# Turning every normed row tile of the later quarters by DMA from two queues, with three more weight units held in SBUF, in a recurrent-memory attention plus MLP kernel

## The chip, the core and the metric

One core of a Trainium2 chip. The metric is the device time of one execution in microseconds (us). Engines are named as in the profile: PE (TensorE; PEld is its weight loads), DVE (VectorE), ACT (ScalarE), POOL (GpSimd) and SP (SyncE, which here only issues DMAs). ACTq, SPq and POOLq are the rows of the DMA issues and waits of these engines' instruction streams.

## The reference, cut to what matters

```python
xn = layernorm(x)                                    # x: 2048 x 1024, bf16
mem = mem0                                           # 8 x 1024
for s in range(64):                                  # 64 segments of 32 rows
    h = concat(mem, xn[32*s : 32*s+32])              # 40 rows
    q, k, v = h @ Wq, h @ Wk, h @ Wv                 # 32 heads of 128
    p = softmax(mask(q @ k.T / sqrt(128)))
    o = (p @ v) @ Wo                                 # 40 x 1024
    mem, out[32*s : 32*s+32] = o[:8], o[8:]
out = x + out + gelu(xn @ w1 + b1) @ w2 + b2         # hidden size 3584
```

## The kernel before

**Two parts.** First comes the MLP for all rows, then the 64 segments, which depend on each other through `mem`. The attention weights are cut into 64 units of 512 KB. 47 of them are resident in SBUF, the other 17 of each segment come again every segment (`start_stream`): 15 through DMAs from copies in DRAM (`Wc_...`) into a ring of six SBUF places, two from PSUM banks. A stream slot is filled again as soon as PE is done with it (`unit_done`).

**The MLP goes in four quarters of 512 rows** (`tg` 0 to 3; four row tiles of 128 rows each). A quarter has 28 groups of the first product (`first_product`, L523, eight matmuls each), each followed by the gelu on ACT and DVE (L594, L598 to L602, and `gelu_tail` L582, L583), and then the second product (L643, or L674 in the last quarter): per row tile `t` two groups of 28 matmuls, and after each two additions on DVE (L650, L651). The finished row tile goes to DRAM (`keep_R`, L473).

**The next quarter's input is made beside the second product.** Its four row tiles are normed (`ln_stats`, `ln_sqrt`, `ln_rstd`, `ln_apply`: L401 to L420) and turned, so that the model dimension lies on the partitions; the turned tile pair is `xnT`. The first product of the next quarter reads all four turned tiles at once. In the kernel before, row tiles 1, 2 and 3 are turned by DMA (`send_x`, L448: eight `dma_start_transpose` of 32 x 512 per row tile, all issued by ACT), and row tile 0 by PE (`turn_x`: eight transposes L429, then copies L434 on DVE and ACT), placed on PE between `t` 2 and `t` 3. `ln_xn` has two buffers, so the third tile's `ln_apply` waits until the first tile's DMAs have read it.

**Order.** Every engine's order is the order written in the program (a manual schedule); the layer below only puts in semaphore waits, by the regions of SBUF and DRAM that instructions read and write. On SP stand, at the end of a quarter: the four `keep_R`, the loads of x for the quarter after next, in quarter 0 the copies of the streamed units to DRAM and the first five resident units (`EARLY`), then `keep_xT` (L456, L466; the latter wait for POOL's copies L461), then `turn_R` (L510: 52 or 56 small DMAs from DRAM to DRAM that bring the quarter's rows into the segments' layout). `turn_R` is issued by SP in quarters 0 and 1 and by POOL in quarter 2; the last quarter's rows go in pieces during segments 1 to 4.

**Weights during the last quarter.** As `w1`, `w2` and gelu places fall free, units are fetched into them (`fetch_resident`), in the order of `RES_PLACES`. Units that find no place are in `LATE`: five of them (tiles `W_O_...`), fetched in segment 0 one at a time, each behind a streamed unit, as are `xt2` and `xt3`.

**Segment 0** (`first`) has `sums(0)` (the row sums of the softmax) behind unit 7 of the second Q half pass; the others have it behind unit 4.

Of the kernel before, what the change touches and what calls it, by code (L numbers as in the profile page):

```python
# [10 lines left out]
BF16 = mybir.dt.bfloat16  # L11
# [6 lines left out]
P = 128  # L18
S = 2048
DM = 1024  # L20
# [38 lines left out]
SUMS_0 = (4, 4, 4, 4)  # L59
# [59 lines left out]
def kernel(  # L119
# [16 lines left out]
    nc = tc.nc  # L136
# [48 lines left out]
    def slab(place):  # L185
        if place in low:
            return low[place]
        return slabs.tile([P, 2048], BF16, name="u", tag=place)
# [39 lines left out]
    NP1 = FC // 2  # L228
    RING = ["xn0", "xn1", "w1_0", "w1_1", "xn2", "xn3"]
    assert len(RING) == STREAM_BUFS  # L230
    EARLY = list(low) + ["spare0", "spare1"]
    RES_PLACES = EARLY + ["xt0", "xt1"] + [f"w1_{k}" for k in range(2, NP1)]
    for k in range(7):
        RES_PLACES += [f"w2_{2 * k}", f"w2_{2 * k + 1}", f"gT{k}"]
    UNIT_AT = dict(zip(RES_PLACES, RESIDENT))
# [18 lines left out]
    def fetch_resident(*places):  # L254
        for place in places:
            unit = UNIT_AT[place]
            res_tiles[unit] = slab(place)[:, :]
            fetch(res_tiles[unit], unit)
# [88 lines left out]
    with tc.tile_pool(name="ma", bufs=2) as ma:  # L347
# [39 lines left out]
        for i in range(14):  # L387
            t = slab(f"w2_{i}")[:, :].rearrange("p (c d) -> p c d", d=DM)
# [5 lines left out]
        rstd = ma.tile([P, NT], F32, name="ln_rstd", bufs=1)  # L394

        half_stats = {}

        def ln_half(tt, c):
            if c == 0:
# [5 lines left out]
        def ln_stats(tt):  # L405
            ln_half(tt, 0)
            ln_half(tt, 1)

        def ln_sqrt(t0, t1):
            nc.scalar.activation(  # L410
                out=rstd[:, t0:t1], in_=mv[:, t0:t1, 1:2].rearrange("p t o -> p (t o)"), func=ACT.Sqrt,
                bias=eps_t[:, :], scale=1.0,
            )

        def ln_rstd(t0, t1):
            nc.vector.reciprocal(out=rstd[:, t0:t1], in_=rstd[:, t0:t1])

        def ln_apply(tt):
            xn = ma.tile([P, DM], BF16, name="ln_xn")
            nc.vector.tensor_scalar(  # L420
                out=xn[:, :], in0=xtoks[tt], scalar1=mv[:, tt, 0:1], scalar2=rstd[:, tt:tt + 1],
                op0=ALU.subtract, op1=ALU.mult,
            )
            return xn

        def turned(xn):
            pT = new_ps("pT")
            for kt in range(KT):
                nc.tensor.transpose(pT[:, kt, :], xn[:, kt * P:(kt + 1) * P], ident)  # L429
            return pT  # L430

        def turned_out(tt, pT, half, xnT, cp):
            t = tt % 4
            cp(  # L434
                out=xnT[half][:, 4 * t:4 * t + 4, :, :].rearrange("p s k t -> p k s t"),
                in_=pT[:, 4 * half:4 * half + 4, :].rearrange("p k (s t) -> p k s t", t=SEG),
            )

        def turn_x(tt, xn, xnT):
            pT = turned(xn)  # L440
            for half in range(2):
                turned_out(tt, pT, half, xnT, nc.scalar.copy if (tt + half) % 2 else nc.vector.tensor_copy)

        def send_x(t, xn, xnT):

            for i in range(4):
                for half in range(2):
                    nc.scalar.dma_start_transpose(  # L448
                        out=xnT[half][:, 4 * t + i, :, :],
                        in_=xn[SEG * i:SEG * i + SEG, 512 * half:512 * half + 512],  # L450
                    )
# [67 lines left out]
        xnT = new_xnT(0)  # L519
# [47 lines left out]
        for tg in range(4):  # L567
            last = tg == 3
            if last:

                load_x_rows(0)
                load_left_rows(0)
                h = 4 * IN_BANKS[1] + 2 * IN_BANKS[2]
                nc.sync.dma_start(out=kq[:, 0:DM], in_=Wo_v[:, h, :])
                start_stream("xn0")
                start_stream("xn1")
                fetch_resident("xt0", "xt1")
            gts = [slab(f"gT{i}")[:, :].rearrange("p (c t) -> p c t", c=4) for i in range(7)]

            def gelu_tail(fb, u, xb):  # L580
                sg = ma.tile([P, 512], BF16, name="g_sg")
                nc.scalar.activation(out=sg[:, :], in_=u[:, :], func=ACT.Sigmoid, scale=GELU_C)  # L582
                nc.vector.tensor_tensor(out=gts[fb // 4][:, fb % 4, :], in0=sg[:, :], in1=xb[:, :], op=ALU.mult)  # L583

            pend = None
            for fb in range(FC):
                if tg == 0 and fb < len(begun):
                    ps = begun[fb]
                    first_product(ps, fb, xnT, 8, 16)
                else:  # L590
                    ps = new_ps()
                    first_product(ps, fb, xnT, 0, 16)
                xb = ma.tile([P, 512], BF16, name="g_xb", bufs=3)
                nc.scalar.activation(  # L594
                    out=xb[:, :], in_=ps[:, :], func=ACT.Identity, bias=b1col[:, fb:fb + 1], scale=1.0
                )
                u = ma.tile([P, 512], BF16, name="g_u")
                nc.vector.tensor_tensor(out=u[:, :], in0=xb[:, :], in1=xb[:, :], op=ALU.mult)  # L598
                nc.vector.tensor_scalar(
                    out=u[:, :], in0=u[:, :], scalar1=0.044715, scalar2=1.0, op0=ALU.mult, op1=ALU.add  # L600
                )
                nc.vector.tensor_tensor(out=u[:, :], in0=u[:, :], in1=xb[:, :], op=ALU.mult)  # L602
                if pend is not None:
                    gelu_tail(*pend)
                pend = (fb, u, xb)
                if last and fb == MEM_AT:
                    put_mem(o_sb, nxt["hT"], new_ps(), wide=False)
                    nc.sync.dma_start(out=d_oL[:, 0:DM], in_=Wo_v[:, h + 1, :])
                if last and fb % 2:
                    place = f"w1_{fb // 2}"  # L610
                    if place in RING:
                        start_stream(place)
                    else:
                        fetch_resident(place)
            gelu_tail(*pend)

            if tg == 0:
                for nb in range(2):
# [4 lines left out]

            if not last:
                xnT = new_xnT(tg + 1)
                for t in range(4):
                    ln_stats(4 * tg + 4 + t)
                ln_sqrt(4 * tg + 4, 4 * tg + 8)
                ln_rstd(4 * tg + 4, 4 * tg + 8)
                for t in (1, 2):  # L630
                    send_x(t, ln_apply(4 * tg + t + 4), xnT)
                for t in range(4):
                    ttg = 4 * tg + t
                    if t == 1:
                        send_x(3, ln_apply(4 * tg + 7), xnT)
                    if t == 2:
                        xn = ln_apply(4 * tg + 4)
                    rsb = xtoks[ttg]
                    for nb in range(2):
                        cs = slice(nb * 512, (nb + 1) * 512)  # L640
                        ps = new_ps()
                        for fc in range(FC):
                            nc.tensor.matmul(  # L643
                                ps[:, :],
                                lhsT=gts[fc // 4][:, fc % 4, t * P:(t + 1) * P],
                                rhs=w2_sb[fc // 2][:, fc % 2, cs],
                                start=(fc == 0),
                                stop=(fc == FC - 1),
                            )
                        nc.vector.tensor_tensor(out=ps[:, :], in0=ps[:, :], in1=b2bc[:, cs], op=ALU.add)  # L650
                        nc.vector.tensor_tensor(out=rsb[:, cs], in0=ps[:, :], in1=rsb[:, cs], op=ALU.add)  # L651
                        if nb == 1 and t == 2:
                            turn_x(4 * tg + 4, xn, xnT)
                    keep_R(ttg, rsb)
                xtoks.update({tt: load_x(tt) for tt in range(4 * tg + 8, min(4 * tg + 12, NT))})
                if tg == 0:
# [2 lines left out]
                    fetch_resident(*EARLY)  # L659
                keep_xT(tg + 1, xnT)  # L660
                for t in range(4):
                    turn_R(4 * tg + t, nc.gpsimd if tg == 2 else nc.sync)
            else:


# [51 lines left out]
    with tc.tile_pool(name="late", bufs=1) as late:  # L717
# [66 lines left out]
        for s in range(NSEG):  # L784
            g, i4 = divmod(s, GRP)
            first, final = s == 0, s + 1 == NSEG
# [113 lines left out]
            def q_left(u):  # L900

                if i4 >= 2 + u and more:
                    q = qS[:, i4 - 2 - u, :, :]
                else:
                    q = qL[u][:, :, NL * i4:NL * i4 + NL]
                nc.vector.tensor_copy(out=q_home[:, :, 0:NL], in_=q)
# [197 lines left out]
            at = {} if first else {1: [lambda: q_left(0)]}  # L1104
# [7 lines left out]
            if left_q[0] and not first:  # L1112
# [5 lines left out]
            at = {  # L1118
                0: [lambda: nc.vector.transpose(out=nat_home, in_=nat_home)],
            }  # L1120
            at[7 if first else SUMS_0[i4]] = [lambda: sums(0)] + ([] if first else [lambda: q_left(1)])
            if left_q[1] and not first:
                at[0].insert(0, lambda: keep_q(1))
            if left_k[1]:
# [56 lines left out]
            for n, unit in enumerate(O_UNITS):  # L1181
                t = unit_tile(unit)
# [115 lines left out]
```

## Time and profile before

| | |
|---|---|
| Median of 3 runs | 1794.47 us (1789.17 to 1797.13) |
| The profiled execution | 1797.63 us, of which the span of its trace is 1795.9 us |
| MLP | 0 to about 404 us of the span; quarters' first products from about 12, 111.86, 210.05 and 307.19 us |
| Segments | from about 404 us to the end |
| PE busy | 1701.3 us (95%) |
| DVE, ACT, POOL busy | 984.2, 683.8, 300.4 us |
| DMA | 594.43 MB, mean 331 GB/s |

Rows of the trace give start and length in us of an instruction or of a run of equal ones; a number in brackets is the idle time before it, with what ended it. `x24` means 24 instructions. In a table of windows each engine's busy time in the stretch is followed by its count; then come the granted PE clock (1.00 is full speed), the mean busy share of the 16 DMA engines and their GB/s.

### The profile page before, as it was taken

The page shows a single profiled execution, that of the slowest core. Times are in us where ns is not written, and L with a number is a line of the kernel's source. Part 1 is how long each engine was busy: PE and PEld are TensorE (multiplying, and loading weights), DVE is VectorE, ACT ScalarE, POOL GpSimd, SP SyncE. Part 2 cuts the span into 40 slices and gives each one's busy share as a digit, 9 for nine tenths or more (in the row PEclk, how much of TensorE's full clock was granted, in tenths as well). Part 3 has the DMA queues.
Part 4 walks back from the last instruction along what each step waited for, and adds up shares of the span by engine and source line. Part 5 has one row for each costly group of instructions (what it writes and reads, how often), then busy time and mean ns, then how long its engine had stood idle before and what let it go on. Part 6 is the DMA issues. An engine that isn't in the chain of part 4 may idle for free.

```text
span 1795.9 us, 71439 instructions
## 1 busy us (share of the span) xinstructions
PE 1701.3 (95%) x31065; PEld 892.2 (50%) x31085; DVE 984.2 (55%) x2514; ACT 683.8 (38%) x1692; POOL 300.4 (17%) x586
## 2 busy tenths in 40 slices
PE   8999999998998999999999999999999999999998
PEld 4444444444455554555555555454555454555554
DVE  7657483825554555555555555555555555555554
ACT  6334261603333333333333434333334343434333
POOL 0000002401231111111121212111112111111211
PEclk9999999999999999999999999999999999999999
DMA  9455222779999999999999999999999999999998
GB/s 284 137 149 185 73 62 64 258 246 380 377 389 367 368 380 375 387 389 376 387 389 374 386 375 396 378 382 379 385 380 385 380 374 384 394 371 393 390 393 321
DMA packets 232830, 594.43 MB, mean 331 GB/s; under 512 B 57715, under 2 KB 88035, under 8 KB 232516
## 3 DMA queue, kind: packets, MB, share of 16 engines
q1 hardware_dynamic: 197584, 567.08, 84.3%
q0 software_dynamic: 16896, 16.85, 2.9%
q10 hardware_dynamic: 18036, 5.94, 1.3%
q8 instruction: 243, 3.98, 0.9%
q14 instruction: 71, 0.58, 0.1%
HBM read 573.43 MB, written 28.90 MB: 335 GB/s over the span
## 4 chain that ended last, share of the span: by engine, by line
PE 76%; DMA 12%; DVE 4%; ACT 4%; issue 3%; ACTq 1%; POOL 0%; DVEq 0%; POOLq 0%; SPq 0%
PE acc L811 38%; PE acc L1069 13%; PE ps L523 11%; DMA u<-Wc_O 7%; PE ps L643 7%; DMA u<-Wc_V 4%; PE ps L674 3%; ACT mixed L980 1%; PE acc L1020 1%; PE mixed L928 1%; DVE kq L895 1%; ACTq L448 1%; DVE pd_main L993 1%; DMA u<-Wc_K 1%; ACT kq L890 1%
## 5 line engine op out<-in xcount | busy, mean ns | idle before, releaser
L811 PE MATMUL acc<-u,hr_home 128*32 128x512 bf16 x11520 | 761.1, 380 | 18.9 <-issue 10.8
L811 PEld LDWEIGHTS <-hr_home 128*32 128x32 bf16 x12288 | 348.6, 96 | 287.9 <-issue 39.4
L811 PE MATMUL acc<-u,hrL 128*32 128x512 bf16 x2880 | 255.6, 380 | 4.1 <-DVE qL L863 2.0
L523 PE MATMUL ps<-u 128*128 128x512 bf16 (+1 forms) x920 | 196.2, 376 | 0.0
L271 DVE TENSOR_SCALAR u<-kept 128x512 uint32<-128x512 uint32 x254 | 163.2, 685 | 55.5 <-PE acc L811 40.7
L863 ACT CAST d_oL<-acc 128x512 bf16<-128x512 f32 x143 | 82.0, 584 | 264.2 <-PE acc L811 252.1
L1069 PEld LDWEIGHTS <-kq 128*32 128x32 bf16 x3908 | 106.2, 99 | 80.6 <-issue 23.9
L643 PE MATMUL ps<-u 128*128 128x512 bf16 x657 | 145.2, 379 | 0.8
L523 PEld LDWEIGHTS <-u 128*128 128x128 bf16 x920 | 90.5, 99 | 103.6
L1069 PE MATMUL acc<-u,d_oL 128*32 128x512 bf16 x1944 | 133.3, 381 | 7.5 <-DMA u<-Wc_O 4.5
L1069 PE MATMUL acc<-u,kq 128*32 128x256 bf16 (+1 forms) x2372 | 119.9, 319 | 14.4 <-DMA u<-Wc_O 12.2
L993 DVE TENSOR_TENSOR pd_main<-kq,mixed 128x320 bf16<-128x320 bf16 x128 | 62.5, 488 | 128.9 <-ACT mixed L980 127.9
L895 DVE STREAM_TRANSPOSE kq<-kq 128x512 bf16<-128x512 bf16 x128 | 91.0, 711 | 72.5 <-ACT kq L890 70.5
L890 ACT CAST kq<-acc 128x512 bf16<-128x512 f32 (+2 forms) x192 | 85.4, 445 | 111.0 <-PE acc L811 81.4
L1260 POOL DMA_DIRECT2D out_dram<-hr_home x168 | 85.4, 516 | 221.6 <-DVE hr_home L1227 221.4
L867 ACT CAST kq<-acc 128x512 bf16<-128x512 f32 x128 | 75.2, 588 | 111.7 <-PE mixed L934 109.9
L811 PEld LDWEIGHTS <-hrL 128*32 128x32 bf16 x3072 | 88.4, 96 | 58.2 <-issue 5.0
L958 DVE TENSOR_TENSOR kq<-kq,mixed 128x96 bf16<-128x96 bf16 (+1 forms) x256 | 38.1, 190 | 121.6 <-ACT kq L948 67.8
L643 PEld LDWEIGHTS <-u 128*128 128x128 bf16 x672 | 65.5, 98 | 78.8 <-DVE g_u L602 0.4
L594 ACT ACTIVATE g_xb<-ps,b1col 128x512 bf16<-128x512 f32 x112 | 76.8, 686 | 71.0 <-PE ps L523 70.4
L980 ACT ACTIVATE mixed<-mixed,small_consts 128x160 f32<-128x160 f32 x256 | 94.2, 368 | 8.4
L1069 PEld LDWEIGHTS <-d_oL 128*32 128x32 bf16 x2592 | 66.5, 96 | 62.2 <-issue 16.8
(127 smaller groups left out, 1987.6 us busy)
## 6 DMA issues: line engine op xcount, KB each, us to landing
u<-Wc_K SPq DMA_DIRECT2D x256, 512.0 KB
u<-Wc_V SPq DMA_DIRECT2D x256, 512.0 KB
u<-Wc_O SPq DMA_DIRECT2D x256, 512.0 KB
u<-Wc_Q SPq DMA_DIRECT2D x192, 512.0 KB
u<-in_B_w_dram SPq DMA_DIRECT2D x28, 512.0 KB
u<-in_A_Wq_dram SPq DMA_DIRECT2D x13, 512.0 KB
u<-in_A_Wv_dram SPq DMA_DIRECT2D x12, 512.0 KB
u<-in_A_Wk_dram SPq DMA_DIRECT2D x9, 512.0 KB
```

Source lines behind the costliest of these rows:

```text
L271: nc.vector.tensor_single_scalar(out=out, in_=in_, scalar=0, op=ALU.bitwise_or)
L523: nc.tensor.matmul(ps[:, SEG * s0:SEG * s1].rearrange("p (s t) -> p s t", t=SEG), lhsT=w1_sb[fb // 2][:, kt, (fb % 2) * P:(fb % 2 + 1) * P ...
L594: nc.scalar.activation(out=xb[:, :], in_=ps[:, :], func=ACT.Identity, bias=b1col[:, fb:fb + 1], scale=1.0)
L643: nc.tensor.matmul(ps[:, :], lhsT=gts[fc // 4][:, fc % 4, t * P:(t + 1) * P], rhs=w2_sb[fc // 2][:, fc % 2, cs], start=(fc == 0), stop=(fc ...
L811: nc.tensor.matmul(o, lhsT=lhs[:, i, :], rhs=m, start=(i == seq[0]), stop=(i == seq[-1]), tile_position=(0, 32 * j),)
L863: cp(out=out, in_=ps.rearrange("p (h e) -> p h e", e=32))
L890: nc.scalar.copy(out=q_home[:, h0:h1, NL:40], in_=ps[:, 32 * h0:32 * h1].rearrange("p (h e) -> p h e", e=32))
L895: nc.vector.transpose(out=home, in_=home)
L980: nc.scalar.activation(out=mixed[:, 160 * b:160 * b + 160], in_=mixed[:, 0:160], func=ACT.Exp, scale=-1.0, bias=off[:, b:b + 1],)
L993: nc.vector.tensor_tensor(out=pdA.rearrange("p c b q -> p b c q"), in0=prA[:, None, :, :].to_broadcast([P, 2, 4, 40]), in1=dd, op=ALU.mult,)
L1069: nc.tensor.matmul(acc[r0:r0 + rows, 0:256 * len(blocks)], lhsT=lhsT, skip_group_check=True, rhs=o_columns(t, k, blocks), start=start, sto ...
L1260: loads.dma_start(out=out_flat[rows, 256 * j:256 * j + 256], in_=res[32 * j:32 * j + NX, :])
```

## The change

- All four row tiles of quarters 1 to 3 are turned by DMA. `send_x` takes the engine that issues: tiles 0 and 2 from SP, tiles 1 and 3 from ACT. `turn_x`, with its PE transposes and its copies, is gone (the first quarter keeps its own turning by PE).
- Statistics, square root and reciprocal go by pairs of row tiles. Tile 0 is sent behind the first square root, tile 1 behind both; tiles 2 and 3 are normed and sent in front of `t` 1 and `t` 2 of the second product.
- The normed tiles and the gelu's small tiles lie in three 4 KB slabs (`late2`, `late0`, `late1`) that later hold weight units. So 43 instead of 40 units have a place of `RES_PLACES`, and `LATE` has two units instead of five. `late2` is fetched early in the last quarter, `late0` and `late1` behind its last gelu. `g_xb` has four buffers instead of three.
- `turn_R` is issued by POOL in quarters 0 and 1 too.
- `sums(0)` of segment 0 stands behind unit 4 instead of 7.

```diff
-    RES_PLACES = EARLY + ["xt0", "xt1"] + [f"w1_{k}" for k in range(2, NP1)]
+    RES_PLACES = EARLY + ["late2", "xt0", "xt1"] + [f"w1_{k}" for k in range(2, NP1)] + ["late0", "late1"]
...
+        xn_place = slab("late2")
+        xns = deque(xn_place[:, DM * k:DM * k + DM] for k in range(2))
+        small_places = [slab("late0"), slab("late1")]
+        parts = [small_places[k // 4][:, 512 * (k % 4):512 * (k % 4) + 512] for k in range(8)]
+        xbs, us, sgs = deque(parts[0:4]), deque(parts[4:6]), deque(parts[6:8])
...
-            xn = ma.tile([P, DM], BF16, name="ln_xn")
+            xn = next_of(xns)
...
-        def turn_x(tt, xn, xnT):
-            pT = turned(xn)
-            for half in range(2):
-                turned_out(tt, pT, half, xnT, nc.scalar.copy if (tt + half) % 2 else nc.vector.tensor_copy)
-
-        def send_x(t, xn, xnT):
+        def send_x(t, xn, xnT, eng):
             for i in range(4):
                 for half in range(2):
-                    nc.scalar.dma_start_transpose(
+                    eng.dma_start_transpose(
                         out=xnT[half][:, 4 * t + i, :, :],
                         in_=xn[SEG * i:SEG * i + SEG, 512 * half:512 * half + 512],
                     )
...
-                fetch_resident("xt0", "xt1")
+                fetch_resident("late2", "xt0", "xt1")
...
             gelu_tail(*pend)
+            if last:
+                fetch_resident("late0", "late1")
...
-                for t in range(4):
-                    ln_stats(4 * tg + 4 + t)
-                ln_sqrt(4 * tg + 4, 4 * tg + 8)
-                ln_rstd(4 * tg + 4, 4 * tg + 8)
-                for t in (1, 2):
-                    send_x(t, ln_apply(4 * tg + t + 4), xnT)
+                t0 = 4 * tg + 4
+
+                def norms(a):
+                    for tt in range(t0 + a, t0 + a + 2):
+                        ln_stats(tt)
+                    ln_sqrt(t0 + a, t0 + a + 2)
+                    ln_rstd(t0 + a, t0 + a + 2)
+
+                norms(0)
+                send_x(0, ln_apply(t0), xnT, nc.sync)
+                xn = ln_apply(t0 + 1)
+                norms(2)
+                send_x(1, xn, xnT, nc.scalar)
                 for t in range(4):
                     ttg = 4 * tg + t
-                    if t == 1:
-                        send_x(3, ln_apply(4 * tg + 7), xnT)
-                    if t == 2:
-                        xn = ln_apply(4 * tg + 4)
+                    if t in (1, 2):
+                        send_x(t + 1, ln_apply(t0 + t + 1), xnT, (nc.sync, nc.scalar)[t - 1])
...
-                        if nb == 1 and t == 2:
-                            turn_x(4 * tg + 4, xn, xnT)
...
-                    turn_R(4 * tg + t, nc.gpsimd if tg == 2 else nc.sync)
+                    turn_R(4 * tg + t, nc.gpsimd)
...
-            at[7 if first else SUMS_0[i4]] = [lambda: sums(0)] + ([] if first else [lambda: q_left(1)])
+            at[4 if first else SUMS_0[i4]] = [lambda: sums(0)] + ([] if first else [lambda: q_left(1)])
```

More of the change, by code (lines that the diff above doesn't have):

```diff
@@ L396, with next_of @@
         half_stats = {}
+        xn_place = slab("late2")
[3 more added lines that the diff above has]
+        xbs, us, sgs = deque(parts[0:4]), deque(parts[4:6]), deque(parts[6:8])
+        def next_of(ring):
+            ring.rotate(-1)
+            return ring[-1]
         def ln_half(tt, c):
@@ L576 @@
                 start_stream("xn1")
-                fetch_resident("xt0", "xt1")
+                fetch_resident("late2", "xt0", "xt1")
             gts = [slab(f"gT{i}")[:, :].rearrange("p (c t) -> p c t", c=4) for i in range(7)]
             def gelu_tail(fb, u, xb):
-                sg = ma.tile([P, 512], BF16, name="g_sg")
+                sg = next_of(sgs)
                 nc.scalar.activation(out=sg[:, :], in_=u[:, :], func=ACT.Sigmoid, scale=GELU_C)
@@ L592 @@
                     first_product(ps, fb, xnT, 0, 16)
-                xb = ma.tile([P, 512], BF16, name="g_xb", bufs=3)
+                xb = next_of(xbs)
                 nc.scalar.activation(
@@ L596 @@
                 )
-                u = ma.tile([P, 512], BF16, name="g_u")
+                u = next_of(us)
                 nc.vector.tensor_tensor(out=u[:, :], in0=xb[:, :], in1=xb[:, :], op=ALU.mult)
```

## The prediction

> **What bounds the kernel now.** I read the page's slices first, then windows around the end of the MLP, then the timeline at each quarter's end. Every chance below is against 0.5%, about 9 us, which is what a measurement of this kernel can tell from no change.
>
> ```profile
> PE   8999999998998999999999999999999999999998
> ...
> DMA  9455222779999999999999999999999999999998
> ```
> ```profile
> 345.00:360.00 15.00, 14.95 (x70) 6.84 (x70) 12.68 (x35) 9.07 (x15) 8.39 (x16) 1.00 0.66 197
> 360.00:404.00 44.00, 43.79 (x202) 19.86 (x203) 11.46 (x17) 1.17 (x2) 1.67 (x3) 1.00 0.72 244
> ...
> 412.00:440.00 28.00, 23.59 (x482) 12.46 (x478) 13.71 (x33) 6.69 (x20) 5.12 (x10) 0.94 1.04 401
> ```
> The columns behind the stretch are PE, PEld, DVE, ACT and POOL busy, clock, DMA share, GB/s. In the MLP (first nine slices) PE alone is full: 14.95 of 15 and 43.79 of 44 us, with a third of the DMA time free. From 412 us on it is the other way: DMA share 1.04 at 401 GB/s, PE 4.4 us idle of 28; later windows show a share of 0.99 to 1.01 up to 1700 us. So an MLP delay moves the end one for one, and bytes taken out of the segments shorten them. Now the first quarter's end, in order of time:
>
> ```profile
> 63.05 36.43 PE L643 MATMUL ps<-u 128*128 128x512 bf16 x164
> ...
> 68.36 0.21 DVE L403 BATCH_NORM_AGGREGATE ln_mv<-ln_stats 128x2 f32<-128x12 f32 x1
> ...
> 72.52 32.10 ACTq L448 DMA_TRANSPOSE u<-ln_xn  x24
> ...
> 84.05 0.55 DVE L420 TENSOR_SCALAR ln_xn<-u,ln_mv,ln_rstd 128x1024 bf16<-128x1024 bf16 x1 [7.27 <-DMA u<-ln_xn]
> ...
> 94.41 0.55 DVE L420 TENSOR_SCALAR ln_xn<-u,ln_mv,ln_rstd 128x1024 bf16<-128x1024 bf16 x1 [5.55 <-DMA u<-ln_xn]
> ...
> 99.77 12.25 PE L643 MATMUL ps<-u 128*128 128x512 bf16 x55
> ...
> 111.86 2.32 PE L523 MATMUL ps<-u 128*128 128x512 bf16 x10
> ```
> Three tiles' 24 DMA turns take 32.1 us of ACT's queue and end at 104.6 us, 7 us before PE wants them. The third and fourth L420 waited for a buffer, so 84.05 and 94.41 are when the first and the second tile had been read and landed.
>
> **Part 1: four turns in a row instead of three in a stream.** One turn:
>
> ```profile
> L448 ACTq DMA_TRANSPOSE u<-ln_xn x1: 1257/1257/1257, 81.6 to 81.6; - x1
> ```
> This is the eighth issue, from the trace in a window of 0.5 us: it ends at 82.9, 10.3 us behind the first, and its landing is seen at 84.05. So a tile takes 11.5 us from first issue to landing (third quarter: 268.53 to 279.96, 11.4). In one queue the next tile doesn't wait for that landing: 94.41 less 84.05 is 10.4.
>
> In the changed kernel's built order the first transpose of each later tile waits for all eight DMA semaphores, that is for the landing of the tile before it, because it is issued from the other queue. The four turns then stand one behind another: 4 x 11.5, and three hand-overs through eight semaphore waits of 17 ns, 0.15 each: 46.5 us. The trace of before has one stream only and can't show two. The Trainium skill, page "DMA: Bandwidth & Descriptors", section "Silent corruption: two transposing streams in flight at once", speaks against this change: the later stream's first transpose must wait for the earlier stream's full completion count. By that rule the wait can't be removed and the sum is the one made here; if the two queues ran side by side, as no run here shows, all tiles would be there some 23 us earlier and this part would cost nothing.
>
> The chain starts earlier than before, as only two tiles are normed first. From the end of the last aggregate to ACT's first issue were 1.16 us (71.36 to 72.52); the second aggregate ends at 68.57, so SP starts at 69.7 and the last tile has landed at 116.2. The first product began at 111.86: 4.3 us later. Second quarter: aggregate end 166.35, start 167.5, landed 214.0 against 210.05: 4.0. Third: 264.55, 265.7, 312.2 against 307.19: 5.0. Sum **13.3 us**. The second product itself would end at 111.6, 208.8 and 307.0, so PE idles 4.6 to 5.2 us each time. Between ends: a turn of 11.1 (landing 0.8 behind the last issue) gives 13.3 - 3 x 1.7 = 8; one of 12.1, as in the second quarter beside other transfers (174.00 to 186.14), gives 13.3 + 3 x 2.4 = 20.5. I take 11.5, seen twice with little else on the queues.
>
> Who stands behind these waits: on SP, `keep_R` of `t` 1 behind tile 2's turns, needed by nothing before the loads that end the quarter; on DVE, the additions of `t` 1 and `t` 2 behind the `ln_apply` of tiles 2 and 3. These wait for tiles 0 and 1, landed at 81.2 and 92.9, while the products they follow end at 81.3 and 93.4 (6.07 us per group from 63.05). PE's six banks give 12 us more, so zero.
>
> **Part 2: what goes.** PE's eight transposes, the wait for their `ln_apply` and the copies: the pause between the two L643 rows is 0.3 us (99.48 to 99.77), 1.3 in the second quarter (196.62 to 197.96), 0.3 in the third: 1.9 us. It isn't taken off, since PE waits for the last tile anyway; it counts only where that wait is hidden.
>
> **Part 3: the clock behind the gap.**
>
> ```profile
> 430.00:434.00 4.00, 2.65 (x52) 1.14 (x48) 2.13 (x6) 1.94 (x6) 0.00 (x0) 1.00 1.05 410
> 434.00:438.00 4.00, 3.31 (x60) 2.37 (x56) 2.12 (x4) 0.74 (x2) 0.00 (x0) 0.63 1.02 392
> ```
> Behind a stretch with PE a third idle the granted clock fell to 0.63 for one window (and 0.95 in the next): 1.7 us lost. Before, no gap between the MLP's quarters is over 1.3 us; now it has three of about 5. Ends 0 and 3 x 1.7 = 5.1; I take half, **2.4**, since the drop comes behind some gaps and not all.
>
> **Part 4: three units fewer in segment 0.** 3 x 0.524 MB at the 401 GB/s of 412 to 440 us: **3.9 us** less DMA work where DMA is the bound. They now go at about 320 us and 357 us, where the shares 0.66 and 0.72 leave room (34% of 15 us is 5 us). Ends: 0, if segment 0 waits for its own chain, and 5.6, if the clock drop at 434 goes too.
>
> **Part 5: the moves that cost nothing.** `turn_R` on POOL: in the third quarter (`tg` 2) POOL already issues 52 of them, from 302.1 to 364.9 us, 560 ns each, while PE is 14.95 of 15 us busy. POOL is next wanted by `keep_xT` about 100 us later. In the first (`tg` 0) they run beside the weight copies (DMA share 0.96 from 120 to 160 us); at twice the length they'd end at about 240 instead of 180, 25 us behind the next `keep_xT` copies, whose rows nobody reads before 315. SP loses 108 issues of 0.6 us and gets 48 transposes; what it carries late is the copies to DRAM, which start behind `keep_R` at the same time as before. `sums(0)` three units earlier: the other segments have it at 4 already; -0.4 to +1 us, taken as 0. The fourth gelu buffer: PE already doesn't wait for gelu, 0.
>
> **Sum.** 13.3 + 2.4 - 3.9 = +11.8. Against the profiled execution, 1797.6 + 11.8 = 1809.4 us; the median of the runs is 3.2 us below that execution, so **1806 us**, +0.65%.
>
> **The rivals.**
> A. *Cheap hand-overs.* Landing is seen 0.8 us behind the last issue and the clock holds: 8 - 3.9 = +4, **1798.5 us**. For it: the clock stood at 1.00 through the MLP's windows, and no trace shows a hand-over between queues. Against it: the eighth issue landed 1.2 us behind its end.
> B. *Slow turns.* POOL's transfers now lie beside the turns of quarters 1 and 2 as SP's did, and all turns take 12.1; each gap costs its 1.7 of clock, and segment 0 gains nothing: 20.5 + 5.1 = +25.6, **1820 us**. For it: the second quarter. Against it: that quarter's first issues also shared SP's semaphores with `turn_R`, which POOL doesn't.
> C. *Not slower: the turns fit under the second product.* It decides at a tile's turn of (111.6 - 69.7) / 4 = 10.5 us: below, PE never waits, part 2's 1.9 come off, and so do the 3.9 of part 4: -5.8, **1788.7 us**; with the clock drop at 434 gone too, 1787. For it: eight issues alone are 10.3 us, so SP and ACT would only have to hide the landing. Against it: 1.2 us of landing, seen by DVE.
> That the change doesn't do what it says is no case: the built order has the transposes on SP and ACT, and 24 transposes fewer on PE.
>
> **How the numbers follow.** Forecast 0.57, A 0.18, B 0.14, C 0.11. The range leaves out C and the far end of B: 1796 to 1819. Slower by over 0.5% means above 1803.4: B and nearly all of the forecast, 0.68. Faster by over 0.5%, below 1785.5, needs C with part 4's far end and more: 0.03. Within: 0.29.
>
> **What would show it.** Right: at each quarter's end four groups of eight DMA_TRANSPOSE, alternately SPq and ACTq, each beginning 11 to 12 us behind the other; PE idle 4 to 6 us ahead of L523 with the release by a DMA; first products beginning near 116, 218 and 321 us (the delays add up). PEclk below 1.00 behind some of these gaps. POOL's L510 rows near 115 to 180 us. From the third quarter's gap to the end about 4 us shorter than before, with DMA still full. Wrong: transposes of both queues overlapping, or no PE gap at the quarters' ends (then C); segments as long as before (then part 4 fails).

## Result and profile after

The changed kernel takes 1818.85 us (median of 6 runs, 1814.87 to 1821.58); the kernel before, run beside it, 1795.8 us. The ratio is 1.0127, 95% interval 1.0093 to 1.0161: 23 us slower, forecast was 12 slower. The profiled execution took 1818.38 us, its span is 1816.7 us, 20.8 longer than before.

Quarters are numbered from 0, as `tg` is. The page's slices show where the time went: in the MLP PE has four slices at 8 where before it had only the first, and the clock has a notch in the third (before, PEclk was 9 in all 40 slices).

```profile
PE   8989899899999999999999899999999999999998
...
PEclk9989999999999999999999999999999999999999
```

The timeline at the end of quarter 0 (start, length, engine, line, operation; L452 is the transposing DMA, L429 `ln_apply`, L527 the first product, L360 the loads of x):

```profile
69.65 10.24 SPq L452 DMA_TRANSPOSE u<-u  x8
...
81.06 34.10 ACTq L452 DMA_TRANSPOSE u<-u  x16
81.06 0.55 DVE L429 TENSOR_SCALAR u<-u,ln_mv,ln_rstd 128x1024 bf16<-128x1024 bf16 x1 [4.34 <-DMA u<-u]
...
92.61 11.04 SPq L452 DMA_TRANSPOSE u<-u  x8
...
113.42 2.74 SPq L360 DMA_DIRECT2D u<-in_A_x_dram  x4
115.56 1.86 PE L527 MATMUL ps<-u 128*128 128x512 bf16 x4 [4.05 <-DMA u<-u]
...
118.64 11.58 PE L527 MATMUL ps<-u 128*128 128x512 bf16 x40 [1.21 <-DMA u<-u]
```

Tile 0 is issued by SP from 69.65 to 79.89 us. ACT's first transpose begins at 81.06, in the same instant in which DVE, released by tile 0's landing, starts its L429: ACT waited for that landing. SP starts tile 2 at 92.61, and ACT's row merges its two tiles, of which the second begins at 104.88. PE ends its second product at 111.5, stands still for 4.05 us, does four matmuls on the half of `xnT` that is there, and stops again. The other two quarters have gaps of 5.44 and 4.98 us; behind the first of these PE stops again, for 0.48 us, behind the other it doesn't. PE's waits from 60 to 420 us have one line:

```profile
PE ps L527 <- DMA u<-u: 16.2, 5, 5.4
```

And the clock, in windows behind the first gap (stretch; PE, PEld, DVE, ACT, POOL busy; clock, DMA share, GB/s):

```profile
112.00:116.00 4.00, 0.43 (x2) 0.19 (x3) 0.94 (x2) 0.00 (x0) 0.42 (x2) 0.76 0.48 131
116.00:120.00 4.00, 2.79 (x8) 0.77 (x7) 0.00 (x0) 0.00 (x0) 1.57 (x5) 0.50 1.05 309
120.00:124.00 4.00, 4.00 (x11) 1.41 (x10) 1.15 (x3) 0.71 (x2) 1.73 (x4) 0.50 0.96 316
124.00:128.00 4.00, 4.00 (x19) 1.82 (x18) 2.29 (x6) 3.97 (x6) 1.66 (x4) 0.96 0.96 231
```

From 120 to 124 us PE is "full" with 11 matmuls; the next window holds 19. The kernel before had as much DMA traffic in this window, and 21 matmuls at full clock:

```profile
120.00:124.00 4.00, 4.00 (x21) 1.82 (x19) 3.80 (x12) 3.15 (x5) 0.00 (x0) 1.00 0.99 330
```

The trace's clock record has half speed for 10.2, 6.8 and 6.8 us at the three gaps.

**Where the time went**, by the starts of PE's products before and after:

| | before | after | longer |
|---|---|---|---|
| Quarter 0's second product and the wait | first product of quarter 1 from 111.86 | from 115.56 | 3.7 |
| First product of quarter 1 | 111.86 to 160.20 | 115.56 to 168.91 | 5.0 |
| Its second product and the wait | to 210.05 | to 222.86 | 4.1 |
| First product of quarter 2 | to 258.40 | to 273.41 | 2.2 |
| Its second product and the wait | to 307.19 | to 326.90 | 4.7 |
| First product of quarter 3 | to 355.80 | to 378.26 | 2.7 |
| From there to the span's end | 1440.1 | 1438.4 | -1.7 |

The waits are 12.5 us. The three longer first products, 9.9 us, hold the second stops (1.2 and 0.5) and the half clock, 8.2.

### The profile page after: what moved, and what is told of

It is laid out like the page before. It is cut to its first block, busy times and chain, and to the rows that moved or that the text cites. A ratio compares the mean times of both kernels' runs of the same rounds, so it can differ in the third digit from the quotient of the medians.

```text
span 1816.7 us, 71349 instructions
## 1 busy us (share of the span) xinstructions
PE 1706.2 (94%) x31041; PEld 891.7 (49%) x31061; DVE 985.1 (54%) x2514; ACT 682.5 (38%) x1692; POOL 359.2 (20%) x694
## 4 chain that ended last, share of the span: by engine, by line
PE 71%; DMA 16%; DVE 3%; ACT 3%; issue 3%; ACTq 2%; SPq 1%; POOL 0%; DVEq 0%; POOLq 0%
PE acc L820 36%; PE acc L1078 12%; PE ps L527 11%; DMA u<-Wc_O 9%; DMA u<-Wc_V 5%; PE ps L654 5%; PE ps L683 3%; ACTq L452 2%; ACT mixed L989 1%; PE acc L1029 1%; PE mixed L937 1%; DMA u<-u 1%; SPq L452 1%; DVE kq L904 1%; DVE pd_main L1002 1%
## 5 line engine op out<-in xcount | busy, mean ns | idle before, releaser
L820 PE MATMUL acc<-u,hr_home 128*32 128x512 bf16 x11520 | 763.2, 380 | 12.3 <-DMA u<-Wc_V 5.6
L527 PE MATMUL ps<-u 128*128 128x512 bf16 (+1 forms) x920 | 204.5, 386 | 16.2 <-DMA u<-u 16.2
L1078 PE MATMUL acc<-u,d_oL 128*32 128x512 bf16 x2592 | 169.8, 380 | 11.7 <-DMA u<-Wc_O 6.0
L527 PEld LDWEIGHTS <-u 128*128 128x128 bf16 x920 | 92.0, 101 | 127.2 <-issue 25.1
L1078 PE MATMUL acc<-u,kq 128*32 128x256 bf16 (+1 forms) x2884 | 136.0, 310 | 17.2 <-DMA u<-Wc_O 14.2
L598 ACT ACTIVATE u<-ps,b1col 128x512 bf16<-128x512 f32 x112 | 76.8, 686 | 193.4 <-PE ps L527 147.3
```

Source lines behind the costliest of these rows:

```text
L527: nc.tensor.matmul(ps[:, SEG * s0:SEG * s1].rearrange("p (s t) -> p s t", t=SEG), lhsT=w1_sb[fb // 2][:, kt, (fb % 2) * P:(fb % 2 + 1) * P ...
L598: nc.scalar.activation(out=xb[:, :], in_=ps[:, :], func=ACT.Identity, bias=b1col[:, fb:fb + 1], scale=1.0)
L820: nc.tensor.matmul(o, lhsT=lhs[:, i, :], rhs=m, start=(i == seq[0]), stop=(i == seq[-1]), tile_position=(0, 32 * j),)
L1078: nc.tensor.matmul(acc[r0:r0 + rows, 0:256 * len(blocks)], lhsT=lhsT, skip_group_check=True, rhs=o_columns(t, k, blocks), start=start, sto ...
```

## Experiments

Theory H: each change of queue makes the next tile wait for the landing of the tile before, and the MLP's loss is that chain plus the clock that falls behind its gaps. Rivals: a fourth tile turned by DMA is too much by itself; something else of the change slows the MLP. Ratios are to the kernel before, run beside each.

**All four tiles from one queue.**

```diff
-                send_x(1, xn, xnT, nc.scalar)
+                send_x(1, xn, xnT, nc.sync)
...
-                        send_x(t + 1, ln_apply(t0 + t + 1), xnT, (nc.sync, nc.scalar)[t - 1])
+                        send_x(t + 1, ln_apply(t0 + t + 1), xnT, nc.sync)
```

> The changed kernel with all four row tiles' transposes issued by SP (one queue), nothing else different. Theory H (the hand-over between two queues makes the gap: each tile waits for the landing of the one before it): without hand-overs the 32 issues go at 1.29 us each, from 69.7 to about 111.7 us with two R_n writes between them, the last one lands about 113 to 114; the first product begins 1.5 to 2.5 us behind the second product's end (111.5) instead of 4.1, the clock holds in most gaps, and the time is about 1803 us. Rival D (DMA turning of a fourth tile is too long by itself, whatever the queues): the first tile still takes 11.4 us and so does each later one, the gap stays 4 to 5 us at each quarter's end and the time stays at 1818 us.

Measured: 1799.82 us, 1.0016 (0.9992 to 1.0040): 19 of the 23 us are gone with the two hand-overs from SP to ACT and the one back. In the timeline the first two tiles are one run without a pause:

```profile
69.11 20.90 SPq L452 DMA_TRANSPOSE u<-u  x16
...
102.61 10.15 SPq L452 DMA_TRANSPOSE u<-u  x8
...
113.90 47.66 PE L527 MATMUL ps<-u 128*128 128x512 bf16 x220 [0.18 <-DMA u<-u]
```

The gaps are 1.7, 2.3 and 2.0 us, and the clock stays at 1.00 in all of them, as in the window of the first:

```profile
112.00:116.00 4.00, 3.13 (x14) 1.31 (x15) 0.74 (x2) 0.69 (x1) 2.73 (x8) 1.00 0.56 180
```

The first products take 48.7, 48.7 and 48.8 us here, against 53.4, 50.6 and 51.4 in the changed kernel. That is 9 of the 18 us by which the MLP is shorter, 1.5 of them the second stops; the rest is shorter gaps. Rival D falls.

**The turning of before with the rest of the change.** `turn_x` and the loop of before are put back in the changed kernel; its SBUF places, late units, `turn_R` on POOL and `sums(0)` stay.

```diff
+                    if t == 1:
+                        send_x(3, ln_apply(4 * tg + 7), xnT, nc.scalar)
+                    if t == 2:
+                        xn = ln_apply(4 * tg + 4)
...
+                        if nb == 1 and t == 2:
+                            turn_x(4 * tg + 4, xn, xnT)
```

> The changed kernel with the turning of the kernel before (tiles 1 to 3 by DMA from ACT, tile 0 by PE), but with all the rest of the change: normed and gelu tiles in weight slabs, two late units instead of five, turn_R on POOL, sums(0) of segment 0 behind unit 4. Theory H: the turning is the whole loss and the rest gains what the segments gained, 1.6 us by the spans of before and after (1392.4 against 1390.8 us from the end of the second product of the last quarter) up to 4: about 1792 to 1794 us against 1796 of the kernel before, and no gap at the quarters' ends. Rival P (turn_R on POOL, or the slabs, slow the MLP): the first products stay longer than 48.4 us, and it is 1800 us or more.

Measured: 1792.78 us, 0.9979 (0.9961 to 0.9997). The turning is the whole loss, and the rest of the change gains 3.8 us (0.5 to 7.0). First products take 48.35 us as before (111.64 to 159.99), and PE has no gap ahead of them, so POOL's `turn_R` and the slabs cost the MLP nothing:

```profile
111.64 48.51 PE L532 MATMUL ps<-u 128*128 128x512 bf16 x224
159.99 36.42 PE L654 MATMUL ps<-u 128*128 128x512 bf16 x168
```

**PE kept at work through the gap.** These 24 matmuls write a PSUM bank that nobody reads.

```diff
+                ps = new_ps()
+                for _ in range(24):
+                    nc.tensor.matmul(ps[:, :], lhsT=w2_sb[0][:, 0, 0:P], rhs=w2_sb[0][:, 0, 0:512], start=True, stop=True)
                 xtoks.update({tt: load_x(tt) for tt in range(4 * tg + 8, min(4 * tg + 12, NT))})
```

> The changed kernel with 24 matmuls of 128x512 that nobody reads put on PE behind each second product of the first three quarters (24 x 0.216 = 5.2 us, the length of the gap). They add no data that anything waits for. Theory K (the lost clock is a term of its own, 8.4 us by the half-speed stretches of the trace: 3.8, 1.7 and 2.9): the clock stays at 1.00 through the three gaps, the first products take 48.4 us plus the wait for the second half, and the time falls by 6 to 8 us to about 1811 to 1813. Rival: the first products are slow because of the DMA traffic or late data; then they stay at 53, 50.5 and 51 us and the time stays at 1818 or gets longer by the overrun, up to 2 us.

Measured: 1810.70 us, 1.0087 (1.0058 to 1.0116): 8 us less than the changed kernel by the medians, though the two intervals overlap. The window that held 0.50 before now has

```profile
116.00:120.00 4.00, 2.44 (x11) 0.82 (x10) 0.00 (x0) 0.00 (x0) 1.30 (x5) 1.00 1.01 281
```

and the first products of quarters 1 and 3 are 3.4 and 2.6 us shorter. At the end of quarter 1 the tile came 2.2 us behind the last of the 24 matmuls, and one window of half speed (3.4 us in the clock record) followed this gap:

```profile
222.78 50.35 PE L527 MATMUL ps<-u 128*128 128x512 bf16 x224 [2.21 <-issue]
```

In this one trace the MLP is only 2.8 us shorter: the 24 matmuls put the first product of quarter 1 1.4 us later, and that of quarter 2 began 2.0 us later behind the start of quarter 1's second product. So the clock is a term of its own: in the two first products where it was kept, some 6 of the table's 8.2 us are gone. What this is worth in the whole time isn't pinned down to better than some us.

**The loads of x behind the last landing.**

```diff
+                keep_xT(tg + 1, xnT)
                 xtoks.update({tt: load_x(tt) for tt in range(4 * tg + 8, min(4 * tg + 12, NT))})
...
-                keep_xT(tg + 1, xnT)
```

> The changed kernel with the loads of x (four of 256 KB on SP) put behind keep_xT, so that they are issued only when the last tile has landed. Theory L (the second stop of PE, 1.2 us at 117.4 and 0.5 us at 224.7, is the last transposes' landing held up by these loads): both stops go, the last transposes land 1.2 instead of 3.4 us behind their issue, and the time falls by 1.7 us and by up to 1.7 us more where the clock comes back a window sooner: about 1815 to 1817. Rival: the landing behind ACT's last issue is late by itself; then the stops stay and the time is 1818 to 1819.

Measured: 1813.42 us, 1.0104 (1.0075 to 1.0132). Both second stops are gone; the first products are one run each:

```profile
114.86 50.19 PE L527 MATMUL ps<-u 128*128 128x512 bf16 x224 [4.04 <-DMA u<-u]
...
218.38 50.05 PE L527 MATMUL ps<-u 128*128 128x512 bf16 x224 [4.97 <-DMA u<-u]
```

That is 5 us less by the medians, though the two intervals overlap, and 5.2 by the start of the last quarter's second product (373.09 against 378.26): 3.3 in quarter 1's first product, where the half clock is one window instead of three, and 0.7 in quarter 2's; 0.7 is an earlier start at 69 us. The 1 MB of loads held the landing of the last transposes up. The edit moves quarter 0's copies to DRAM behind that landing too; but at the end of quarter 1, which has loads of x alone, the stop is gone as well, and the end of quarter 2, which has no loads of x, shows no second stop in either kernel.

**More hand-overs.** The issuing engine goes by the 32-row piece `i` of a tile instead of by the tile.

```diff
-                    eng.dma_start_transpose(
+                    (nc.sync, nc.scalar)[i % 2].dma_start_transpose(
```

> The changed kernel with the queue changing behind every two transposes (SP, ACT, SP, ACT within each tile), 15 hand-overs per quarter instead of 3. Theory H: each hand-over costs the landing behind the last issue, 1.2 us, and the waits, 0.15; 12 more per quarter put the last landing 14 to 16 us later, PE idles 18 to 21 us per quarter end instead of 4 to 5, and the time is 3 x 15 = 45 us longer, about 1864 us. Rival (only the number of transposes counts): 1818 us.

Measured: 1838.34 us, 1.0229 (1.0196 to 1.0262): 19.5 us more than the changed kernel, not 45. The expectation counted 15 changes of queue per quarter from the source. In the trace the queue changes one by one in tile 0 and by fours later, 11 times in each quarter; why the order isn't that of the source, no view shows. For 24 more hand-overs in all, PE's wait grew from 16.2 to 40.4 us:

```profile
PE ps L527 <- DMA u<-u: 40.4, 3, 15.6
```

24.2 / 24 = 1.0 us each, against 1.17 from 79.89 to 81.06 in the changed kernel. So the price per hand-over holds, and with the number of transposes equal it is the number of hand-overs that sets the wait.

**An earlier start, two queues and one.** Row tile 0 is normed and sent beside the last gelu groups, tiles 1 to 3 behind the gelu with one square root.

```diff
+                if not last and fb == 22:
+                    ln_stats(4 * tg + 4)
+                if not last and fb == 24:
+                    ln_sqrt(4 * tg + 4, 4 * tg + 5)
+                if not last and fb == 25:
+                    nxt_T = new_xnT(tg + 1)
+                    ln_rstd(4 * tg + 4, 4 * tg + 5)
+                    send_x(0, ln_apply(4 * tg + 4), nxt_T, nc.sync)
```

> The same earlier start, but the tiles alternate between SP and ACT as in the changed kernel (tile 0 SP, 1 ACT, 2 SP, 3 ACT), so the hand-overs are all there. Theory H: a turn still takes 11.5 us from tile to tile, tile 1 starts at about 74 and tile 3 has landed at about 108.5 us, 3 us ahead of PE: the hand-overs cost nothing and the time is that of e5_early_one_queue, about 1792 us. Rival Q (transposes from two queues slow the kernel in another way, by ACT's queue or by the transfers): slower than e5 by more than 3 us.

Measured: 1792.62 us, 0.9975 (0.9955 to 0.9994). The hand-overs are there, the gap isn't:

```profile
64.51 10.75 SPq L452 DMA_TRANSPOSE u<-u  x8
...
76.47 33.94 ACTq L452 DMA_TRANSPOSE u<-u  x16
...
88.00 10.89 SPq L452 DMA_TRANSPOSE u<-u  x8
...
111.16 48.51 PE L527 MATMUL ps<-u 128*128 128x512 bf16 x224
```

Tile 1 waits for tile 0's landing until 76.5 (not for its norm, as I had expected at 74), and ACT's last issue ends at 110.4, 0.8 us ahead of PE's first matmul; the margin is thin.

The same start with all four tiles on `nc.sync`:

> All four tiles turned from SP's queue as in e1_one_queue, and row tile 0 normed and sent already beside the last gelu groups of the quarter before (statistics behind group 22, its square root behind group 24, sent behind group 25), tiles 1 to 3 normed together behind the gelu. Theory H: tile 0 lands before about 73 us, tiles 1 to 3 go from about 74 us in one stream of 32 us and have landed by 107 us, 4 us ahead of PE; no gap at the quarters' ends, quarters of 96.9 us (48.4 + 48.5) against 97.1 of e2_old_turning and 99.0 of e1_one_queue: about 1791 to 1792 us, the fastest so far. Rival: the earlier norm holds up the gelu (DVE has 0.17 us to spare per group and gets 2 us more), PE waits for the last gelu in the second product, 1 to 3 us per quarter: 1794 to 1800 us.

Measured: 1792.55 us, 0.9990 (0.9961 to 1.0018). As in the two-queue version PE has no gap at the quarters' ends; of the rival's wait for the last gelu there is 0.2 us, in quarter 2's second product. Its interval reaches 1, so which of this, the two-queue version and the old turning is fastest stays open; the medians lie within 0.3 us. Two of them, with intervals below 1, beat both kernels.

**The price of a unit in the segments.** The old-turning kernel loads a resident unit over itself in twelve segments.

```diff
+            if 5 <= s < 20 and i4:
+                again = next(unit for unit in RESIDENT if unit[0] == "Q" and unit[2] == 0)
+                fetch(res_tiles[again], again)
             psV, psVL = half_pass("V", 0, left_v[0], {})
```

> e2_old_turning with twelve more loads of 512 KB on SP, one in each of twelve segments between 5 and 19 (a resident unit of Q is loaded over itself at the start of the V passes; the data are the same). It prices one unit of DMA work in the segments, on which part 4 of the prediction rests. Theory B (DMA is the bound and every unit moves the end by 0.524 MB / 382 GB/s = 1.37 us): 12 x 1.37 = 16.5 us more than e2_old_turning, about 1809 us. Rival (PE's own chain is as long as DMA's, and a unit more is partly hidden): under 8 us more, below 1801 us.

Measured: 1805.51 us, 1.0054 (1.0027 to 1.0080): 0.0075 above the old-turning kernel, 13.5 us for twelve units, 1.1 us each. That is nearer to the full DMA price of 1.37 than to the rival's 0.7 or less, but the two intervals together leave some 8 to 19 us, 0.6 to 1.6 a unit.

## Why the prediction was right, and where it was mis-sized

**Part 1, the chain of turns: right, its fit in part by luck.** Predicted turns of 11.5 and hand-overs of 0.15 more; measured starts at 69.65, 81.06, 92.61 and 104.88, steps of 11.4 to 12.3. Predicted landings at 116.2, and later starts of 4.3, 4.0 and 5.0 (13.3); measured 3.7, 4.1, 4.7 (12.5). By the Trainium skill's rule on two transposing streams ("DMA: Bandwidth & Descriptors", section "Silent corruption: two transposing streams in flight at once") the later stream's first transpose must wait for the earlier one's full completion; the trace agrees, 81.06 being the instant of that landing, and the one-queue kernel shows what the wait costs. The luck: I let PE wait for the whole last tile, but PE began on one half of `xnT`. The whole tile had landed 48.9, 48.9 and 47.1 us behind a quarter's first issue, where I had 46.5.

**What part 1 left out: the second stop, 1.7 us in all.** I let the loads of x cost nothing since they come behind the quarter. But SP issued them from 113.4 us, while the last transposes were in flight, and the last landing came 3.4 us behind its issue (115.16 to about 118.6) instead of 1.2. Moved back, they gave 5 us, more than the stop, as the clock came back sooner. Part of this is where the gap lay: the clock fell at 114.05 us in the changed kernel, 1.5 us ahead of PE's return, and at 115.72 with the loads moved, 0.9 us behind it.

**Part 3, the clock: the mis-sized term.** I took half of 1.7 us per gap, 2.4 in all, and 5.1 as the far end; the first products show 8.2. Two things were wrong. "Half the gaps": all three gaps of 4.1 to 5.4 us were followed by half speed. And "one window of 1.7 us": the row that I priced it by, 0.63 in one window behind a stretch of partial work, has one window of half speed, while the gaps of the changed kernel have two or three (10.2, 6.8, 6.8 us), part of it in the gap itself. The Trainium skill, page "TensorE: Matmul & The Clock Gate", section "Part 1: The HAM clock gate (the "warmup" mystery)", has half speed after at least one idle window of about 3.4 us and full speed after a busy one. The traces agree in the window: the three lengths are 3, 2 and 2 times 3.41 us, and the three falls (114.05, 219.86 and 325.68 us) lie 31 times 3.41 us apart. They don't show that the window must be wholly idle. The 3.41 us ahead of the three falls held 2.5, 2.4 and 3.4 us of idle PE, and with PE kept at work a window with the gap of 2.2 us was enough. In the one-queue kernel the gaps of 1.7 to 2.3 us left the clock alone; counted back from its one fall, at the end of the trace, no window of its MLP held more than 1.7 us of idle PE. So by these traces the idle time within one window decides, and where a gap lies counts beside its length.

**Part 4, three units fewer in segment 0: sign and rough size right.** Predicted -3.9; the rest of the change gained 3.8 (0.5 to 7.0) with the old turning, and a unit's price of 1.1 us would give 3.4. The single traces can't show it: from the last second product to the end they have 1432.7 to 1442.5 us for the same segment code. The sign that I named, some 4 us less from the third gap to the end, isn't there: 1489.8 us from 326.90 on, against 1488.7 before, with 2.7 of quarter 3's first product in it. The half clock near 435 us, my far end, is in the trace of before and has no counterpart in that of the changed kernel; whether the change took it away isn't shown. How much of the 3.8 `sums(0)` or `turn_R` had wasn't tried apart.

**Part 5, the moves at nothing: right** for `turn_R`, the slabs and the fourth gelu buffer (first products of 48.35 us with them). POOL's first `turn_R` took from 119.3 to 186 us, not to the 240 that I allowed.

**The sum.** 12.5 + 1.7 + 8.2 - 3.8 = 18.6, against 23 by the medians with an interval of 16.7 to 28.9. The side was right. That the range, up to 1819 us, held the median of 1818.85 is luck: three of the six runs lie above it. The forecast of +12 was half of the change; of the 11 us that lacked, 5.8 are the clock and 0.9 the waits with the second stop, and some 4 stand in no term; the interval leaves as much open. Rival B's 1820 us came out nearly right by other sums: its gaps were to be 20.5 us and were 14.2 with the second stops, its clock 5.1 and was 8.2, and its zero gain in the segments didn't come. Rival C's mechanism, turns that fit under the second product, was what the early versions built.

## What to carry to other kernels

Count changes of queue among transposing DMAs before counting transposes: each of the nine changes here put 1.2 to 1.5 us between one issue and the next, so all of them belong on one queue, or early enough that the chain ends before PE asks. A PE gap must be priced in two parts, its length and the half clock behind it; the six gaps of 4.0 to 5.4 us in two of these kernels cost 1.5 to 3.8 us more behind them, while of four gaps near 2 us three (1.7, 2.0 and 2.3) cost 0.4 at most and one (2.2) cost 1.8. And what is issued next to a transfer that PE is about to wait for, here 1 MB of loads for a later quarter, delays that transfer.

## What the runs showed of the hardware that I hadn't expected

A landing behind the last transposing DMA is 1.2 us alone and 3.4 us with 1 MB of loads issued 1.7 us before its issue ended. The half clock lasted 10.2 us where PE came back in pieces (four matmuls, a stop of 1.2 us, then the rest) and 3.4 us behind a gap of the same 4 us without the stop, which also lay otherwise to the windows of 3.41 us. At the quarters' ends of all these kernels, each such window at full clock with 2.2 us or more of idle PE was followed by half speed, and none with 1.7 us or less was.
